# A fused attention and two-MoE kernel: k of the fourth head pair is turned by VectorE, two small opening steps change places or engines, and the last store changes its queue

## The chip, the cores and the metric

The kernel runs on one core of a Trainium2 chip. The time is device microseconds of one execution. Three executions of the kernel before took 952.24, 953.11 and 955.57 us; the median is 953.11 us.

## The reference

There are three stages. First, causal attention with a decay, over 4 batches, 8 heads, 576 positions and a head dimension of 64; then two feed-forward blocks on the 2304 by 512 result.

```
scores = q @ k.T / sqrt(64)
cum    = cumsum(log(clip(f, 1e-4, 1)))            # f: one forget factor per head and position
scores = where(causal, -1e9, scores + cum_i - cum_j)
attn   = softmax(scores);  x = attn @ v           # x becomes 2304 x 512
x      = relu(x @ w_in)**2 @ w_out                # 512 -> 2048 -> 512
out    = (sigmoid(x @ w_gate) * (x @ w_val)) @ w_out2   # 512 -> 1536 -> 512
```

## The kernel before

The 32 heads are worked in 16 pairs (p = 0 to 15), two heads side by side on the 128 partitions. Each fp32 operand is split into a high and a low part, and each product is a sum of matmuls of such parts. q and k must stand with the head dimension on the partitions. For q, TensorE transposes five 128x128 blocks into PSUM (step TQ). For k there are two ways, chosen by the constant TP. Pairs below TP load k as it is, TensorE transposes it (step TK) and ScalarE and VectorE make its high and low part from PSUM (kh and kl "late"). Pairs from TP on load k by four DMAs (L294) that already put 32x32 blocks where they belong; VectorE turns the blocks in place with one instruction (step TKv, L494), and ScalarE and GpSimd make the parts (steps khe and kle). Before the change TP is 4.

The attention is a pipeline written out by hand. The list ORDER (L647) names the steps of one iteration, each with a lag: a step with lag -1 works in iteration `it` on pair it+1. Two tables, `ahead` and `behind` (L675 to 697), hang further work on a step of an iteration. Every engine runs its instructions in that order, and SyncE issues all DMAs in it. PSUM is a ring of four tiles (`ps2`, names pa0 to pa3, two banks each): every transposing step, score step and product takes the next tile of the ring, and waits until the tile's former user is done. TQ takes an extra tile for k where p is below TP (L454).

The steps that matter here, in short: ql and kl make the low parts of q and k on VectorE; S2, S3, S01 and S4 are the score matmuls (L439, L545); R is the row minimum on VectorE (L413), X the exponential on ScalarE (L421), M the scaling on GpSimd (L565); G is the transposing of the weights on TensorE (L576, L582), E its copy out of PSUM; PV is the product with v (L610). In `setup` (L336) f is clamped, its logarithm taken on ScalarE, summed by a scan on VectorE, and split in two parts that are stored in SBUF and sent by DMA (cr_load, L311) to the rows that the score matmuls read.

When the last pairs run out, TensorE fills its gaps with the first four groups of the up product (`fill_mm`, L661, two groups to a ring tile, one in each bank); `up1_post` on ScalarE reads each (Relu, L234; Square, L235). Then the eight PSUM banks are used singly (`hbank`, L730), from bank 0 on, which is the first half of pa0.

At the end, `finish2` (L1502) adds the last products and stores three pieces of the last rows; all by SyncE.

Of the kernel before, what the change touches and what calls it, by code (L numbers as in the profile page):

```python
# [13 lines left out]
AF = mybir.ActivationFunctionType  # L14
ALU = mybir.AluOpType
# [26 lines left out]
def kernel(  # L42
# [13 lines left out]
    nc = tc.nc  # L56
    B, H, S, D = q.shape
# [211 lines left out]
    cum_f = pts[0:BH, 0:S]  # L269
    f_sb = pts[0:BH, S:2 * S]  # L270
    cum_s = pts[0:BH, 2 * S:5 * S].bitcast(F32R)
# [1 line left out]
    cum_b = pts[0:BH, 6 * S:6 * S + 3 * HALF].bitcast(BF16)  # L273

    ring = [0]
    TP = 4

    def k_flat(p):
        return nat["k"][p % 2].rearrange("p c h d -> p (c h d)")[:, 0:S]
# [1 line left out]
    def ps2():  # L281
        ring[0] += 1
        return pair_t[(ring[0] - 1) % 4]

    def load(p, which):
        b, h0 = divmod(2 * p, H)
        for src, nm_ in ((q, "q"), (k, "k"), (v, "v")):
            if nm_ not in which:
                continue
            t = nat[nm_][p % len(nat[nm_])]  # L290
            if nm_ == "k" and p >= TP:
                for r in range(4):
# [43 lines left out]
    def setup():  # L336
        nc.vector.memset(qk[1]["kh"].bitcast(F32)[:, 0:256], 0.0)
        nc.vector.memset(one_l.bitcast(F32), 0.0)
        for r in range(2):
            nc.vector.memset(one_l.bitcast(F32)[64 * r:64 * r + 64, 128 * r:128 * r + 128], 1.0)  # L340
        nc.vector.memset(cum_s.bitcast(F32)[:, 2 * S:3 * S], 0.0)
        for t in sm_t:
            nc.vector.memset(t[:, 9:13], 1.0e-9)
        nc.vector.memset(nm_t[0][:, 9:11], 0.0)
        for r in range(2):
            nc.vector.memset(nm_t[0][64 * r:64 * r + 64, 9 + r:10 + r], 1.0)
        busy(16)
        nc.sync.dma_start(out=f_sb, in_=f.rearrange("b h s -> (b h) s"))
        make_identity(nc, ident)
        for nm_ in "qk":  # L350
            for t in nat[nm_]:
                nc.gpsimd.memset(t[64:128, NF, :, :], 0.0)
        load(0, "qk")
        nc.vector.tensor_reduce(out=nm_t[0][:, 0:1], in_=ident[:, 0:111:22], axis=mybir.AxisListType.X, op=ALU.add)
        nc.vector.tensor_scalar(one_l, one_l.bitcast(F32), nm_t[0][:, 0:1], None, op0=ALU.mult)
        nc.vector.tensor_scalar(f_sb, f_sb, 1.0e-4, 1.0, op0=ALU.max, op1=ALU.min)
        nc.scalar.activation(out=f_sb, in_=f_sb, func=AF.Ln)
        nc.scalar.activation(out=sm_t[0][0:BH, 0:1], in_=f_sb[:, 0:1], func=AF.Exp)
        nc.vector.tensor_tensor_scan(out=cum_f, data0=f_sb, data1=f_sb, initial=0.0, op0=ALU.add, op1=ALU.min)
        nc.scalar.activation(out=cum_s[:, 0:S], in_=cum_f, func=AF.Copy)  # L360
        nc.vector.tensor_tensor(
            out=cum_s[:, S:2 * S], in0=cum_f, in1=cum_s.bitcast(F32)[:, 0:S], op=ALU.subtract
        )
        for d in qk:
            nc.gpsimd.memset(d["cr"].bitcast(F32), 0.0)
        for t in nat["v"]:
            nc.gpsimd.memset(t[64:128, NF, :, :], 0.0)
        for t in pt_t:
            nc.gpsimd.memset(t[:, 2 * POFF[NF] + S:2 * POFF[NF] + PC], 0.0)
        cum_v = cum_s.bitcast(F32).rearrange("p (t s) -> p t s", t=3)  # L370
        load(1, "q")
        cr_load(0, cum_v)
        load(1, "k")
        cr_load(1, cum_v)
        nc.gpsimd.memset(maskc, 0.0)
        nc.gpsimd.affine_select(
            out=maskc[:, MD:MD + 128], in_=maskc[:, MD:MD + 128], pattern=[[-1, 128]],
            compare_op=ALU.is_ge, fill=BIG, base=0, channel_multiplier=1,
        )
        for r in range(2):  # L380
            nc.gpsimd.affine_select(
                out=maskc[64 * r:64 * r + 64, S - REM:S], in_=maskc[64 * r:64 * r + 64, S - REM:S],
                pattern=[[-1, REM]], compare_op=ALU.is_ge, fill=BIG, base=0, channel_multiplier=1,
            )
# [67 lines left out]
    def TQ(p):  # L452
        x = ps2()
        if p < TP:  # L454
            live["kt", p] = ps2()
# [29 lines left out]
    def TK(p):  # L485
        if p >= TP:
            return
# [2 lines left out]
            load(p + 2, "k")  # L490

    def TKv(p, first=False):
        if p >= TP and first == (p < TP + 2):
            nc.vector.transpose(out=k_flat(p), in_=k_flat(p))  # L494
            live["k", p] = k_flat(p)

# [141 lines left out]
    for c in range(9):  # L638
        t = "4" if c == 8 else f"{c // 2}{'ab'[c % 2]}"
# [36 lines left out]
    for m in range(2):  # L676
# [5 lines left out]
        for n in range(4):  # L682
            ahead[b + 6 + n if m == 0 else b + 6, "kle"] = (
                ahead.get((b + 6, "kle"), []) * m + [part_fn(conv_low, m, n)]
            )
    for p in range(TP, TP + 2):
        behind[p - 2, "N0"] = [lambda p=p: TKv(p, True)]
    behind[2, "TK"] = [lambda: w_load("in", 0), lambda: w_load("in", 1)]
    behind[-1, "TQ"] = [lambda: busy(3)]
# [14 lines left out]
    for it in range(min(lags), NP + max(lags)):  # L704
# [6 lines left out]
        for nm_, lag in steps:  # L711
            p = it - lag
# [317 lines left out]
    for i, (k_, jj, w) in enumerate(steps):  # L1030
        if i == NW - 1:
# [12 lines left out]
            for n in range(4):  # L1044
                t = pu_p.tile([128, 4, BT], F32, tag=f"pa{n}", name=f"pa{n}")
# [39 lines left out]
        ws, s = aop[k_, w], gg.pop(i)  # L1085
# [195 lines left out]
    for n, (z, key, m) in enumerate(items):  # L1281
# [12 lines left out]
        elif m % 2:  # L1294
            at(*slot(z + 6), *[part_fn(w_sum, key, m // 2, x) for x in range(4)])
            for x in range(4):
                p = 42 * (m // 2) + x - 1
# [84 lines left out]
    t = wr_p.tile([128, 3584], F32R, tag="r1", name="r1b")  # L1382
# [119 lines left out]
    def finish2(m):  # L1502
# [2 lines left out]
        last = m == wsteps[-1][0]  # L1505
        tl, th = (j * BT + cs.start for j in (j0, j1))

        def store(t, s, lo, hi):
            nc.sync.dma_start(
                out=out[t:t + 128, 256 * lo:256 * hi], in_=r[:, s + lo:s + hi, :].rearrange("p i n -> p (i n)")  # L1510
            )

# [15 lines left out]

        def p4():
            vadd(r[:, 2], two(m, 0)[:, 1], r[:, 2])  # L1530
            store(th, 2, 0, 1)

        def p34():
            vadd(r[:, 1:3], two(m, 3), r[:, 1:3])
# [116 lines left out]
```

## Time and profile before

| what | value |
|---|---|
| median of three executions | 953.11 us |
| the profiled execution | 953.69 us |
| its span, first to last instruction | 951.9 us |
| TensorE matmul busy | 943.2 us (99%), 6255 instructions |
| VectorE, ScalarE, GpSimd busy | 738.1, 560.2, 339.4 us |
| mean granted clock of TensorE | 0.999 |
| DMA | 160.88 MB, 169 GB/s |

The profiled execution is 1.79 us longer than its span. Times below count from the start of the span. A row of a timeline gives the start, the length, the engine, the line of the kernel, what it did, and in brackets how long the engine was idle before it and what ended that. "SPq" is SyncE's queue of DMA issues: the length is that of the issue, not of the transfer. TensorE's weight loads (PEld) run beside its matmuls (PE).

### The profile page before, as it was taken

What the parts mean: (1) busy time and instruction counts of PE and PEld (TensorE: products, weight loads), DVE (VectorE), ACT (ScalarE), POOL (GpSimd) and SP (SyncE); (2) the same over time, 40 slices, a digit from 0 to 9 for tenths busy, and PEclk for the clock granted to TensorE, in tenths of its full rate; (3) what the DMA queues carried; (4) which work ended last, traced back from release to release, by engine and by line L of the source; (5) the groups of instructions that cost most, each with busy time, mean ns of one, the idle gap of its engine ahead of it and who ended that gap; (6) DMA issues with size and microseconds to landing.
All of it is one profiled execution on the core that took longest, in us unless ns stands there. A gap on an engine that the chain in (4) does not pass through costs nothing.

```text
span 951.9 us, 17958 instructions
## 1 busy us (share of the span) xinstructions
PE 943.2 (99%) x6255; PEld 905.7 (95%) x6255; DVE 738.1 (78%) x1467; ACT 560.2 (59%) x1148; POOL 339.4 (36%) x403
## 2 busy tenths in 40 slices
PE   8999999999999999999999999999999999999998
PEld 7888888999999999999999999999999999889998
DVE  7899998277776775787879989767676777698885
ACT  7899998466555756556556566444445455344332
POOL 7798998012021210055023355634243342300000
PEclk9999999999999999999999999999999999999999
DMA  5744430387878988757766513334333345764441
GB/s 121 169 97 97 89 78 15 115 293 249 266 247 279 311 282 296 208 167 208 226 213 204 176 57 103 117 114 138 114 116 128 127 166 201 265 214 143 151 132 69
DMA packets 173635, 160.88 MB, mean 169 GB/s; under 512 B 80328, under 2 KB 150300, under 8 KB 173544
## 3 DMA queue, kind: packets, MB, share of 16 engines
q1 hardware_dynamic: 173544, 159.74, 55.0%
q8 instruction: 49, 0.80, 0.3%
q14 instruction: 42, 0.34, 0.1%
HBM read 102.93 MB, written 56.73 MB: 168 GB/s over the span
## 4 chain that ended last, share of the span: by engine, by line
PE 89%; DVE 4%; DMA 4%; ACT 1%; issue 1%; POOL 1%; SPq 0%; ACTq 0%; DVEq 0%; POOLq 0%
PE ps L1145 28%; PE ps L226 20%; PE ps L1091 10%; PE ps L1491 9%; PE ps L1367 5%; PE pa L610 5%; PE pa L439 4%; PE pa L576 3%; DMA gl<-g 3%; DVE gg L787 2%; PE pa L545 1%; PE pa L395 1%; PE pa L582 1%; PE pa L226 1%; ACT gg L786 1%
## 5 line engine op out<-in xcount | busy, mean ns | idle before, releaser
L226 PE MATMUL ps<-xT,hl 128*128 128x384 f32 x1104 | 191.5, 334 | 0.0
L226 PEld LDWEIGHTS ps<-xT,hl 128*128 128x128 f32 x1104 | 191.4, 188 | 0.0
L1091 PE MATMUL ps<-gg,ao 128*128 128x384 f32 x1008 | 177.6, 335 | 1.5 <-DVE gg L787 1.4
L1091 PEld LDWEIGHTS ps<-gg,ao 128*128 128x128 f32 x1008 | 174.4, 188 | 4.6 <-DVE gg L787 4.4
L565 POOL TENSOR_TENSOR pt<-pt,sm 128x128 f32<-128x128 f32 (+2 forms) x142 | 104.5, 767 | 17.9 <-DVE sm L557 13.8
L787 DVE TENSOR_TENSOR gg<-gl,gg 128x768 fp32r<-128x768 f32 x78 | 85.2, 1099 | 29.3 <-ACT gg L786 28.8
L1145 PE MATMUL ps<-xT,r 128*128 128x384 f32 x576 | 107.6, 334 | 0.0
L786 ACT ACTIVATE gg<-gl 128x768 fp32r<-128x768 f32 x78 | 65.8, 845 | 65.4 <-DMA gl<-g 36.8
L1145 PEld LDWEIGHTS ps<-xT,r 128*128 128x128 f32 x576 | 100.5, 188 | 0.1
L212 DVE TENSOR_TENSOR gt<-gt 128x384 f32<-128x384 f32 x96 | 53.7, 600 | 58.2 <-ACT gt L235 56.0
L421 ACT ACTIVATE pt<-pt,nm 128x384 f32<-128x384 f32 (+2 forms) x144 | 82.8, 579 | 4.4 <-DVE nm L413 4.4
L413 DVE CUSTOM_DVE_ANT_0 pt<-pa,maskc 128x384 f32<-128x384 f32 (+2 forms) x144 | 67.0, 515 | 1.6 <-PE pa L439 1.6
L183 POOL TENSOR_TENSOR hl<-wf,hl 128x512 fp32r<-128x512 f32 x14 | 18.1, 1292 | 125.4 <-ACT hl L179 125.4
L132 ACT ACTIVATE wtmp<-wraw 128x512 f32<-128x512 f32 x66 | 43.9, 665 | 30.5 <-DMA wraw<-in_moe_w_in_dram 12.4
L849 POOL TENSOR_TENSOR xT<-yt,xT 128x384 fp32r<-128x384 f32 x12 | 17.1, 1430 | 122.9 <-ACT xT L845 119.1
L1145 PE MATMUL ps<-xT,f 128*128 128x384 f32 x288 | 55.7, 334 | 0.0
L1145 PE MATMUL ps<-t,r 128*128 128x384 f32 x288 | 54.1, 334 | 0.0
L235 ACT ACTIVATE gt<-gt 128x384 f32<-128x384 f32 x96 | 50.5, 526 | 3.1
L234 ACT ACTIVATE gt<-ps 128x384 f32<-128x384 f32 x92 | 43.9, 477 | 11.7 <-PE ps L226 11.4
L1145 PEld LDWEIGHTS ps<-xT,f 128*128 128x128 f32 x288 | 50.4, 188 | 0.0
L1145 PEld LDWEIGHTS ps<-t,r 128*128 128x128 f32 x288 | 50.3, 188 | 0.1
L155 DVE SCALAR_TENSOR_TENSOR wtmp<-wraw,wtmp 128x512 int32<-128x512 int32 (+1 forms) x68 | 46.5, 684 | 1.6
(259 smaller groups left out, 1935.5 us busy)
## 6 DMA issues: line engine op xcount, KB each, us to landing
gl<-g SPq DMA_DIRECT2D x90, 384.0 KB
g<-gt SPq DMA_DIRECT2D x168, 192.0 KB
wraw<-in_moe_w_out_dram SPq DMA_DIRECT2D x28, 512.0 KB
x<-g SPq DMA_DIRECT2D x72, 128.0 KB
wraw<-in_moe_w_in_dram SPq DMA_DIRECT2D x16, 512.0 KB
wraw<-in_moe_w_val_dram SPq DMA_DIRECT2D x12, 512.0 KB
g<-pb SPq DMA_DIRECT2D x29, 192.0 KB
wraw<-in_moe_w_gate_dram SPq DMA_DIRECT2D x10, 512.0 KB
```

Source lines behind the costliest of these rows:

```text
L212: nc.vector.tensor_tensor(out=t, in0=a, in1=b_, op=ALU.subtract)
L226: nc.tensor.matmul(h, lhsT=a, rhs=xT[c][:, b_, t0:t0 + BT], start=(c == 0 and i == 0), stop=(c == KD - 1 and i == 2))
L235: nc.scalar.activation(out=r, in_=r, func=AF.Square)
L413: nc.vector.tensor_tensor_reduce(out=o, in0=s, in1=mask, scale=1.0, scalar=3.0e38, op0=ALU.add, op1=ALU.min, accum_out=scol(p, nm_t, c),)
L421: nc.scalar.activation(out=x, in_=x, func=AF.Exp, bias=scol(p, nm_t, c), scale=-1.0, accum_out=scol(p, sm_t, c))
L565: nc.gpsimd.tensor_tensor(out=x, in0=x, in1=scol(p, sm_t, c).to_broadcast([128, e - a]), op=ALU.mult)
L610: nc.tensor.matmul(o[64 * h:64 * h + 64, 512 * half + s - lo:512 * half + hi - lo], lhsT=vn[:, c, h, :], rhs=pts[:, h * PW + c * PS + s:h ...
L786: nc.scalar.activation(out=s[:, 0], in_=t, func=AF.Copy)
L787: nc.vector.tensor_tensor(out=s[:, 1], in0=t, in1=s.bitcast(F32)[:, 0], op=ALU.subtract)
L1091: nc.tensor.matmul(o, lhsT=ws[:, a, u, cs], rhs=s[:, b_, u, :], start=(k_ in (0, 2, 5) and w == u == x == 0), stop=(w == NW - 1 and u == 1 ...
L1145: nc.tensor.matmul(o, lhsT=w[p][:, a, ws], rhs=operand(n, jj, b_, c), start=(first and c == x == 0), stop=(c == 1 and x == 2), skip_group_ ...
L1491: nc.tensor.matmul(o, lhsT=YR[i % 4][:, a, FROM[n]], rhs=b_op(n, u, b_), start=(x == u == y == 0), stop=(u == NU2 - 1 and y == 2), skip_gr ...
```

## The change

There are four edits. The clamp of f stands ahead of two small operations on VectorE. The high part of the decay sums is copied by VectorE instead of ScalarE. TP becomes 3, so the fourth pair (p = 3) goes the way of the block loads, and its turn stands in the plain step TKv of iteration 1, while those of pairs 4 and 5 stay where they were (behind N0). The last of the three final stores is issued by ScalarE.

```diff
--- before.py
+++ after.py
@@ -273,7 +273,7 @@
     cum_b = pts[0:BH, 6 * S:6 * S + 3 * HALF].bitcast(BF16)
 
     ring = [0]
-    TP = 4
+    TP = 3
 
     def k_flat(p):
         return nat["k"][p % 2].rearrange("p c h d -> p (c h d)")[:, 0:S]
@@ -351,13 +351,13 @@
             for t in nat[nm_]:
                 nc.gpsimd.memset(t[64:128, NF, :, :], 0.0)
         load(0, "qk")
+        nc.vector.tensor_scalar(f_sb, f_sb, 1.0e-4, 1.0, op0=ALU.max, op1=ALU.min)
         nc.vector.tensor_reduce(out=nm_t[0][:, 0:1], in_=ident[:, 0:111:22], axis=mybir.AxisListType.X, op=ALU.add)
         nc.vector.tensor_scalar(one_l, one_l.bitcast(F32), nm_t[0][:, 0:1], None, op0=ALU.mult)
-        nc.vector.tensor_scalar(f_sb, f_sb, 1.0e-4, 1.0, op0=ALU.max, op1=ALU.min)
         nc.scalar.activation(out=f_sb, in_=f_sb, func=AF.Ln)
         nc.scalar.activation(out=sm_t[0][0:BH, 0:1], in_=f_sb[:, 0:1], func=AF.Exp)
         nc.vector.tensor_tensor_scan(out=cum_f, data0=f_sb, data1=f_sb, initial=0.0, op0=ALU.add, op1=ALU.min)
-        nc.scalar.activation(out=cum_s[:, 0:S], in_=cum_f, func=AF.Copy)
+        nc.vector.tensor_copy(cum_s[:, 0:S], cum_f)
         nc.vector.tensor_tensor(
             out=cum_s[:, S:2 * S], in0=cum_f, in1=cum_s.bitcast(F32)[:, 0:S], op=ALU.subtract
         )
@@ -490,7 +490,7 @@
             load(p + 2, "k")
 
     def TKv(p, first=False):
-        if p >= TP and first == (p < TP + 2):
+        if p >= TP and first == (TP < p < TP + 3):
             nc.vector.transpose(out=k_flat(p), in_=k_flat(p))
             live["k", p] = k_flat(p)
 
@@ -683,7 +683,7 @@
             ahead[b + 6 + n if m == 0 else b + 6, "kle"] = (
                 ahead.get((b + 6, "kle"), []) * m + [part_fn(conv_low, m, n)]
             )
-    for p in range(TP, TP + 2):
+    for p in range(TP + 1, TP + 3):
         behind[p - 2, "N0"] = [lambda p=p: TKv(p, True)]
     behind[2, "TK"] = [lambda: w_load("in", 0), lambda: w_load("in", 1)]
     behind[-1, "TQ"] = [lambda: busy(3)]
@@ -1505,8 +1505,8 @@
         last = m == wsteps[-1][0]
         tl, th = (j * BT + cs.start for j in (j0, j1))
 
-        def store(t, s, lo, hi):
-            nc.sync.dma_start(
+        def store(t, s, lo, hi, eng=nc.sync):
+            eng.dma_start(
                 out=out[t:t + 128, 256 * lo:256 * hi], in_=r[:, s + lo:s + hi, :].rearrange("p i n -> p (i n)")
             )
 
@@ -1528,7 +1528,7 @@
 
         def p4():
             vadd(r[:, 2], two(m, 0)[:, 1], r[:, 2])
-            store(th, 2, 0, 1)
+            store(th, 2, 0, 1, nc.scalar)
 
         def p34():
             vadd(r[:, 1:3], two(m, 3), r[:, 1:3])
```

On VectorE, in iteration 1, between the row minima of pair 1 and the low part of q of pair 2, the change puts this (kn_155 is the tile of k of odd pairs, ql_160 and kl_162 the low parts of pair 2, pt_174 the scores of pair 1):

```order
 L413 ISA pt_174,nm_179<-pa_146,maskc 128x128
 L413 ISA nm_179 128x1
+L494 STREAM_TRANSPOSE kn_155<-kn_155 128x576
 L468 SCALAR_TENSOR_TENSOR ql_160<-pa_147,qh_159 128x576
 L504 TENSOR_TENSOR kl_162<-pa_148,kh_161 128x576
```

One instruction is added; it waits for the four DMAs that load k of pair 3, and ql and kl of pair 2 now stand behind it.

On SyncE, the loads of iterations 0 and 1 (cr_163 is the decay row of pair 2, vn_157 is v of pair 1):

```order
 L304 DMA qn_153<-in_q_dram 64x2x64
 L311 DMA cr_163<-cum_d 6x576
-L300 DMA kn_155<-in_k_dram 128x4x64 x2
-L304 DMA kn_155<-in_k_dram 64x2x64
+L294 DMA kn_155<-in_k_dram 32x18x32 x4
 L300 DMA vn_157<-in_v_dram 128x4x64 x2
 L304 DMA vn_157<-in_v_dram 64x2x64
```

Three issues for k of pair 3 become four; their place in the queue stays the same.

On TensorE, where the fill groups end and the first group in a single bank begins (pa_145 and pa_146 are pa0 and pa1 of the ring, ps_2684 before and ps_2681 now are bank 0). Before:

```order
L226 MATMUL pa_146<-xT_127,hl 128x384 x3
L226 MATMUL pa_146<-xT_128,hl 128x384 x3
L226 MATMUL pa_146<-xT_129,hl 128x384 x3
L226 MATMUL ps_2684<-xT_126,hl 128x384 [waits DVE_49,PE_49]
L226 MATMUL ps_2684<-xT_126,hl 128x384 x2
```

and now:

```order
L226 MATMUL pa_145<-xT_127,hl 128x384 x3
L226 MATMUL pa_145<-xT_128,hl 128x384 x3
L226 MATMUL pa_145<-xT_129,hl 128x384 x3
L226 MATMUL ps_2681<-xT_126,hl 128x384 [waits PE_49,Activation_49]
L226 MATMUL ps_2681<-xT_126,hl 128x384 x2
```

With one ring tile less taken, everything from iteration 2 on sits one tile lower, and the fill groups now lie in pa0, whose first bank is bank 0. The first group there waits for ScalarE now; the count that it waits for is that of the second Relu of the two fill groups.

## Rows read from the trace of the kernel before

**Rows 1.** Chain that ended last, whole run: start us, length us, what worked.

```profile
7.54 2.37 DMA cr<-pts
...
19.09 3.15 POOL pt L565 x3
...
30.70 2.18 PE pa L576 x20
...
177.82 191.36 PE ps L226 x1104
```

**Rows 2.** Busy time by engine in iterations two and three of attention; PEclk is granted clock.

```profile
core 0: us, PE busy (x) PEld busy (x) DVE busy (x) ACT busy (x) POOL busy (x), PEclk, DMA share, GB/s
22.98:33.37 10.39, 10.39 (x106) 8.93 (x106) 8.66 (x29) 8.14 (x25) 7.30 (x11) 1.00 0.69 146
33.37:43.10 9.73, 9.73 (x99) 8.27 (x99) 8.88 (x31) 8.87 (x26) 8.18 (x11) 1.00 0.78 194
```

**Rows 3.** Timeline, VectorE, 16 to 46 us: start, length, line, what; idle before in brackets.

```profile
19.28 0.75 DVE L468 SCALAR_TENSOR_TENSOR ql<-pa,qh 128x576 fp32r<-128x576 f32 x1
...
20.62 0.75 DVE L413 CUSTOM_DVE_ANT_0 pt<-pa,maskc 128x576 f32<-128x576 f32 x1
...
21.29 0.95 DVE L449 COPY pts<-pa 128x768 f32<-128x768 f32 x1
...
33.68 0.78 DVE L494 STREAM_TRANSPOSE kn<-kn 128x576 f32<-128x576 f32 x1
```

**Rows 4.** Timeline, SyncE's DMA issues, 0 to 45 us.

```profile
7.54 0.82 SPq L311 DMA_DIRECT2D cr<-pts  x1
...
13.86 0.61 SPq L304 DMA_DIRECT2D kn<-in_k_dram  x1
...
21.19 0.97 SPq L300 DMA_DIRECT2D kn<-in_k_dram  x2
...
26.67 2.16 SPq L294 DMA_DIRECT2D kn<-in_k_dram  x4
```

**Rows 5.** Timeline, TensorE, 16 to 46 us.

```profile
17.31 0.74 PE L395 MATMUL pa<-ident,kn 128*128 128x128 f32 x5 [0.18 <-DMA kn<-in_k_dram]
...
19.52 2.40 PE L576 MATMUL pa<-ident,pt 128*128 128x128 f32 x20 [0.21 <-DVE nm L413]
...
22.98 0.50 PE L439 MATMUL pa<-cr,one_l 64*128 64x512 f32 x2
```

**Rows 6.** TensorE after its last matmul: stretch, length, busy, granted clock, DMA share, GB/s.

```profile
950.40:950.60 0.20, 0.00 (x0) 0.83 0.63 205
950.60:950.80 0.20, 0.00 (x0) 0.50 0.01 0
```

**Rows 7.** Timeline, TensorE, opening and end of the run.

```profile
1.19 3.78 PE L334 MATMUL pa<-kh 128*128 128x256 f32 x16 [1.19 <-DVE kh L337]
...
944.60 2.28 PE L1491 MATMUL ps<-xT,xT 128*128 128x256 f32 x18
...
947.43 0.87 PE L1491 MATMUL ps<-xT,xT 128*128 128x256 f32 x6
```

**Rows 8.** Timeline, VectorE and ScalarE, opening.

```profile
2.85 0.16 DVE L354 TENSOR_REDUCE nm<-ident 128x1 f32<-128x6 f32 x1
...
3.32 0.54 DVE L356 TENSOR_SCALAR pts<-pts 32x576 f32<-32x576 f32 x1
...
6.00 0.67 ACT L360 ACTIVATE pts<-pts 32x576 fp32r<-32x576 f32 x1
```

**Rows 9.** Timeline, ScalarE, 172 to 181 us.

```profile
177.86 0.49 ACT L234 ACTIVATE gt<-pa 128x384 f32<-128x384 f32 x1 [3.64 <-PE pa L226]
...
178.82 0.47 ACT L234 ACTIVATE gt<-pa 128x384 f32<-128x384 f32 x1
```

**Rows 10.** Tail: last DMA issue on SyncE, and a stretch with its DMA share.

```profile
949.00 0.40 SPq L1509 DMA_DIRECT2D out_dram<-r  x1
...
949.50:950.00 0.50, 0.00 (x0) 0.00 (x0) 0.00 (x0) 0.00 (x0) 0.00 (x0) 1.00 1.04 389
```

## The prediction

> **What bounds the kernel now.** I read the share of busy time first: TensorE is busy for 943.2 of 951.9 us, so a change pays only where TensorE waits or where it has work taken away. Then the chain of waits, in order of time: it runs through TensorE nearly everywhere, from 177.82 us on in one piece of 191.36 us [rows 1]. Only in the opening does it run elsewhere: over the DMA that carries the decay sums (cr, 7.54 us, 2.37 us long) and later over GpSimd's scaling (19.09 us) [rows 1]. All four edits touch the opening, the hand-over to the up product, or the tail. Third, the stretches of iterations 2 and 3: TensorE is busy throughout in both, but iteration 2 takes 10.39 us and iteration 3 takes 9.73 [rows 2]. The difference is the five transposes of k of pair 3. Last, the timelines of VectorE and SyncE around 20 us, because both engines work strictly in order and the change puts a new wait there [rows 3, 4].
>
> The sum is made against the profiled execution, 953.69 us, which lies 0.58 us above the median of 953.11. I take 0.58 off at the end.
>
> **Opening: clamp and copy.** The clamp starts at 3.32 us; two small operations ahead of it start at 2.85 [rows 8]. Ahead of them it gains 0.47 us, if f has landed by then; if f lands only at 3.32, it gains nothing. The copy takes ScalarE 0.67 us [rows 8]. VectorE's price for a copy of this shape isn't in the trace; the clamp on the same 32x576 costs it 0.54 us, which is my value, and a copy as slow as ScalarE's is the other bound. With the hand-over between engines gone this is about 0.13 to 0.2 us. So the issue of cr on SyncE comes 0 to 0.65 us earlier; I take 0.6. SyncE's timeline shows one issue after another, with gaps of 0.1 us at most, from there to the row at 21.19 us [rows 4], so its whole queue moves up by the same 0.6 us. By itself this would be worth 0.6 us. It isn't booked by itself, since the next part decides when TensorE goes on.
>
> **k of pair 3: the new wait.** VectorE reaches the new turn where it began ql of pair 2, at 19.28 us [rows 3], now 18.7. The turn needs the four DMAs of k of pair 3. Their place in SyncE's queue is that of the issue at 21.19 us; four issues of this kind take 2.16 us [rows 4]. So the last issue ends at 21.19 - 0.6 + 2.16 = 22.75. From the end of an issue to the landing the nearest rows give two bounds. cr: 2.37 - 0.82 = 1.55 us [rows 1, 4]. k of pair 2: its last issue ended at 14.47, and TensorE waited for it until 17.31, which makes 2.84 at most [rows 4, 5]. I take 1.7, near cr, since the row of 2.84 may hold other waits too. The landing is then at 24.45, and VectorE stands for some 5.7 us.
>
> Behind the turn on VectorE are ql, kl, the row minimum R4 and the copy E2. In the trace they follow each other by 0.67 us (19.28, then 20.62 and 21.29) [rows 3]. The turn takes 0.78 us [rows 3], so ql ends at 24.45 + 0.78 + 0.75 = 25.98, kl at 26.65, R4 at 27.3. The TensorE steps wait for them through the ring: G2 takes the tile that ql reads, G3 the tile of kl, G4 the tile of R4. So TensorE ends G1 at about 19.6 (start 19.52 - 0.6 [rows 5], six transposes) and stands until 26.0. At 0.109 us for a transpose (2.18 us for 20 [rows 1]) G2 (6), G3 (8, from 26.65) and G4 (5) end at 28.05. Then S3 of pair 1 starts, which started at 22.98 [rows 5]: 5.1 us late.
>
> **The clock after the wait.** TensorE's last matmul ends at 947.43 + 0.87 = 948.30 [rows 7]; the granted clock goes from 1.00 to 0.50, the 1.2 GHz level, around 950.5 [rows 6]. That is 2.2 us of standing; here it stands for 6.4. So I expect G2 to start at half the clock. In the opening, after standing, 16 dummy matmuls of 256 columns took 3.78 us, 0.236 each; at the end 18 of the same width took 2.28 us, 0.127 each [rows 7]. About 3.8 us of half pace is therefore my value for the way back. At 0.218 us for a transpose G2 ends at 27.3, G3 at 29.05, and with the clock back at 29.8 G4 ends at 30.0. S3 is 7.0 us late instead of 5.1; the half clock costs 1.9 us. Its bounds are 0 and, if it stays low through S3 and S2 as well, some 3 us.
>
> The Trainium skill (TensorE: Matmul & The Clock Gate, part 1 on the clock gate) says that the ramp costs under one per cent of a usual kernel and shouldn't be fitted. By that page the term is left out and the whole sum below is 1.9 us smaller; I weigh it as the first rival, at full clock, worked out from the rows above.
>
> **k of pair 3: what goes.** Iteration 2 loses five transposes and becomes like iteration 3: 9.73 - 10.39 = -0.66 us [rows 2]. ScalarE's kh moves to an earlier slot at the same price. GpSimd gets kl of pair 3; it is busy for 7.30 of 10.39 us, and iteration 3 shows the same work done beside a full TensorE at 8.18 of 9.73 [rows 2], so I cost it at nothing. Without that cover it would be under 1 us. The load of k of pair 5 now stands behind two weight loads on SyncE. SyncE can go on issuing while TensorE stands for 6 us, so I cost this at nothing; without the stand it could make VectorE wait, at most for about the 2.16 us of its four issues.
>
> **The ring at the hand-over to the up product.** One ring tile less is taken, so all later tiles shift by one. The last fill groups now lie in pa0, and the first group in single banks (bank 0) waits for ScalarE to read both. Before, this group began at 177.82 without a wait [rows 1]. ScalarE starts the first Relu at 177.86, after waiting for TensorE, and the second at 178.82 for 0.47 us [rows 9]. So TensorE now stands from 177.82 to about 179.3: +1.5 us, in a stage where TensorE has no gap that could take it up. If the first Relu were enough, it would be 0.55; these are the bounds. It is too short to lower the clock by the row above.
>
> **The last store.** SyncE issues it at 949.00 for 0.40 us [rows 10]. ScalarE is idle and could issue 0.2 us earlier; that would give -0.24 with the spacing. But from 949.5 on the 16 DMA engines are at a share of 1.04 [rows 10], busy with the two stores before, so the last byte doesn't come sooner. I take 0, with -0.4 (the whole issue) and +0.4 (an issue as long as cr's 0.82) as bounds.
>
> The Trainium skill (DMA: Bandwidth & Descriptors, "Issuing engines are not separate DMA queues") says that another issuing engine saves only the time of the issue, since all use the same 16 engines. By the issue rows alone this edit gives -0.24, by the page and the share of 1.04 it gives 0; I go by the latter.
>
> **The sum.** +7.0 (S3 late) - 0.66 (transposes) + 1.5 (ring) + 0 (store) = +7.85. 953.69 + 7.85 - 0.58 = 960.95, say 961.0 us.
>
> **Rivals.**
> - The same wait, at full clock: 5.1 - 0.66 + 1.5 = +5.95, which gives 959.05 us. For it: the mean granted clock is 0.999 over the whole run, the opening included, so the opening's slow matmuls are an indirect witness. Against it: the fall at 950.5.
> - A late landing: 2.84 us instead of 1.7, and SyncE's queue doesn't move up by 0.6. That adds 1.75: 962.7 us. For it: 128-byte pieces of k, four times 576 of them. Against it: cr landed in 1.55.
> - No wait (not slower): k of pair 3 lands before VectorE comes to it. Then the opening gives -0.6, the transposes -0.66, the ring +1.5: +0.24, 953.35 us. It decides from a landing at 18.7 us; the issue would have to end at 17.2, and SyncE would have to be 6 us ahead of its trace. Nothing in the rows allows that, unless VectorE were as late itself.
>
> **How the numbers follow.** Forecast 0.55, full clock 0.24, late landing 0.12, no wait 0.07, anything else 0.02. About 0.3% (2.9 us) is what a measurement of this kernel can tell from no change. The first three cases lie above 956.0, so slower has 0.92 with half of the rest; no wait is "same"; for faster, the opening and the transposes would have to be joined by 1.6 us more. The range goes from full clock with the near landing (1.55) and one Relu, 959.05 - 0.15 - 0.95 = 957.95, taken down to 957.0 for an edge of the store and of the opening, up to the late landing with the store's bound, 963.1, taken to 963.5.
>
> **What would show it.** VectorE idle for 5 to 6 us before L494 around 24 us, ended by the DMA of kn; TensorE idle for about 6 us before L576, then a granted clock of 0.5 in the slices from some 22 to 30 us; S3 of pair 1 at 30 us; iterations from 2 on at 9.73 us each; TensorE idle for 1.5 us before the first matmul on ps, ended by ScalarE's L234; DMA share at 1.0 in the last two us as before. I am wrong if VectorE doesn't wait at L494, or if the wait ends at another time than 24 to 26 us; the clock term is wrong if G2 to G4 take 2.1 us instead of 4; the ring term if the first ps matmul follows the fill group at once.

## The result and the profile after

The changed kernel takes 960.32 us (median of 6 executions, 959.68 to 961.12) beside 954.13 us of the kernel before on the same chip. The ratio is 1.0067, with a 95% interval from 1.0051 to 1.0083: slower by 4.9 to 7.9 us. Run once more on another chip it took 959.15 us beside 952.86, ratio 1.0065 (1.0052 to 1.0078). The forecast was 961.0 us. The profiled execution took 961.12 us, with a span of 959.3.

VectorE's timeline after, the rows that answer to [rows 3]:

```profile
18.45 0.08 DVE L413 DVE_READ_ACCUMULATOR2_ANT nm<- 128x1 f32 x1
24.46 0.78 DVE L494 STREAM_TRANSPOSE kn<-kn 128x576 f32<-128x576 f32 x1 [5.92 <-DMA kn<-in_k_dram]
25.16 0.72 DVE L468 SCALAR_TENSOR_TENSOR ql<-pa,qh 128x576 fp32r<-128x576 f32 x1
25.80 0.74 DVE L504 TENSOR_TENSOR kl<-pa,kh 128x576 fp32r<-128x576 f32 x1
27.63 0.96 DVE L449 COPY pts<-pa 128x768 f32<-128x768 f32 x1 [0.41 <-issue]
```

VectorE is free at 18.53 us and stands for 5.92 us before the turn of k of pair 3, until the DMA has brought it. ql, kl and the copy behind it start 5.9 to 6.3 us later than before.

SyncE's queue after, answering to [rows 4]: the decay sums for pair 2, and the four issues of k of pair 3:

```profile
19.20 0.78 SPq L311 DMA_DIRECT2D cr<-cum_d  x1
20.04 2.04 SPq L294 DMA_DIRECT2D kn<-in_k_dram  x4
```

The load stands behind the same transfers as before. The last issue ends at 22.08 us, and VectorE has the data 2.38 us later.

TensorE's timeline after, answering to [rows 5]:

```profile
18.68 0.85 PE L576 MATMUL pa<-ident,pt 128*128 128x128 f32 x6 [0.21 <-DVE nm L413]
26.03 3.22 PE L576 MATMUL pa<-ident,pt 128*128 128x128 f32 x14 [6.50 <-DVE ql L468]
29.04 1.27 PE L582 MATMUL pa<-ident,pt 128*128 128x128 f32 x5
30.24 0.68 PE L439 MATMUL pa<-cr,one_l 64*128 64x512 f32 x2
```

The wait of VectorE is passed on: after six transposes TensorE stands for 6.50 us, until ql has freed the tile of G2. The score step S3 of pair 1 (last row) starts at 30.24 us instead of 22.98.

The same places as stretches (start:end, length, busy time of PE, PEld, DVE, ACT and POOL with instructions, granted clock, DMA share, GB/s), the last two answering to [rows 2]:

```profile
18.68:26.03 7.35, 0.85 (x7) 0.64 (x7) 1.57 (x3) 2.54 (x11) 2.79 (x4) 0.85 0.69 140
26.03:30.24 4.21, 4.21 (x19) 3.88 (x19) 2.40 (x6) 0.96 (x2) 1.91 (x5) 0.50 0.79 150
30.24:40.27 10.03, 10.03 (x99) 8.56 (x99) 8.13 (x29) 8.34 (x26) 7.47 (x10) 0.98 0.23 51
40.27:50.00 9.73, 9.73 (x99) 8.27 (x100) 8.84 (x31) 8.82 (x26) 8.33 (x12) 1.00 0.85 205
```

In the second stretch the granted clock is 0.50, the level of 1.2 GHz: 19 transposes take 4.21 us. Iteration 2 now takes 10.03 us instead of 10.39, with 99 matmuls like iteration 3; a rest of the half clock lies in it (0.98). From iteration 3 on a pass takes 9.73 us, as before.

TensorE's waits after (total, times, longest), the largest four:

```profile
PE pa L576 <- DVE ql L468: 6.5, 1, 6.5
PE ps L226 <- ACT gt L234: 1.5, 1, 1.5
PE pa L334 <- DVE kh L337: 1.2, 1, 1.2
PE ps L1091 <- DVE gg L787: 1.1, 2, 0.7
```

The second one is the hand-over to the up product, which had no wait before [rows 1]. TensorE there, before and then after:

```profile
177.66 14.55 PE L226 MATMUL ps<-xT,hl 128*128 128x384 f32 x83
```

```profile
185.95 4.26 PE L226 MATMUL ps<-xT,hl 128*128 128x384 f32 x23 [1.51 <-ACT gt L234]
```

ScalarE after, answering to [rows 9]:

```profile
184.48 0.49 ACT L234 ACTIVATE gt<-pa 128x384 f32<-128x384 f32 x1 [3.64 <-PE pa L226]
185.43 0.47 ACT L234 ACTIVATE gt<-pa 128x384 f32<-128x384 f32 x1
```

The first matmul on a single bank starts when the second Relu has read (185.43 + 0.47 = 185.90).

The opening on VectorE after, answering to [rows 8]:

```profile
2.85 0.61 DVE L354 TENSOR_SCALAR pts<-pts 32x576 f32<-32x576 f32 x1
5.59 0.45 DVE L360 CAST pts<-pts 32x576 fp32r<-32x576 f32 x1
```

The clamp starts 0.47 us earlier, and the copy takes 0.45 us instead of ScalarE's 0.67 [rows 8]. The issue of cr, at 7.54 us before [rows 4], is at 6.90.

The end of the program, answering to [rows 10]: ScalarE's queue, and the DMA engines (their share of time is the last column but one):

```profile
956.12 0.38 ACTq L1509 DMA_DIRECT2D out_dram<-r  x1
```

```profile
956.50:957.00 0.50, 0.00 (x0) 0.00 (x0) 0.00 (x0) 0.00 (x0) 0.00 (x0) 1.00 0.82 279
957.00:957.50 0.50, 0.00 (x0) 0.00 (x0) 0.00 (x0) 0.00 (x0) 0.00 (x0) 1.00 1.01 379
```

Going through the starts of the stages, after minus before: S3 of pair 1 +7.26 us, the first matmul on ps 185.95 - 177.66 = +8.3, the first of L1091 377.42 - 369.02 = +8.4, the first of L1145 554.64 - 547.95 = +6.7, the span +7.4. So the stage of L1091 took 1.7 us less than before in these two profiles, and 0.7 us of that was lost again behind L1145. That was in no term of the forecast; the experiments come back to it.

### The profile page after: what moved, and what is told of

Read it like the earlier page. It is cut to its first block, busy times and chain, and to the rows that moved or that the text cites. A ratio compares the mean times of both kernels' runs of the same rounds, so it can differ in the third digit from the quotient of the medians.

```text
span 959.3 us, 17949 instructions
## 1 busy us (share of the span) xinstructions
PE 943.8 (98%) x6250; PEld 907.6 (95%) x6250; DVE 739.4 (77%) x1468; ACT 560.1 (58%) x1147; POOL 341.9 (36%) x404
## 4 chain that ended last, share of the span: by engine, by line
PE 91%; DMA 3%; DVE 2%; ACT 1%; issue 0%; POOL 0%; SPq 0%; ACTq 0%; DVEq 0%; POOLq 0%
PE ps L1145 27%; PE ps L226 20%; PE ps L1091 14%; PE ps L1491 9%; PE pa L610 5%; PE pa L576 4%; PE pa L439 4%; PE ps L1367 4%; DMA gl<-g 3%; PE pa L545 1%; DVE gg L787 1%; PE pa L582 1%; PE pa L226 1%; PE pa L395 1%; ACT gg L786 1%; PE pa L534 1%
## 5 line engine op out<-in xcount | busy, mean ns | idle before, releaser
L1091 PE MATMUL ps<-gg,ao 128*128 128x384 f32 x1008 | 176.1, 335 | 1.3 <-DVE gg L787 1.1
L1091 PEld LDWEIGHTS ps<-gg,ao 128*128 128x128 f32 x1008 | 174.5, 188 | 2.7 <-DVE gg L787 2.6
L1145 PE MATMUL ps<-xT,r 128*128 128x384 f32 x576 | 107.5, 334 | 0.0
L787 DVE TENSOR_TENSOR gg<-gl,gg 128x768 fp32r<-128x768 f32 x78 | 84.4, 1090 | 28.7 <-ACT gg L786 28.3
L786 ACT ACTIVATE gg<-gl 128x768 fp32r<-128x768 f32 x78 | 66.0, 846 | 63.5 <-DMA gl<-g 38.7
L1145 PEld LDWEIGHTS ps<-xT,r 128*128 128x128 f32 x576 | 100.5, 188 | 0.1
L1145 PE MATMUL ps<-xT,f 128*128 128x384 f32 x288 | 55.7, 334 | 0.0
L1145 PE MATMUL ps<-t,r 128*128 128x384 f32 x288 | 54.1, 334 | 0.0
L1145 PEld LDWEIGHTS ps<-xT,f 128*128 128x128 f32 x288 | 50.4, 188 | 0.0
L1145 PEld LDWEIGHTS ps<-t,r 128*128 128x128 f32 x288 | 50.3, 188 | 0.1
```

Source lines behind the costliest of these rows:

```text
L786: nc.scalar.activation(out=s[:, 0], in_=t, func=AF.Copy)
L787: nc.vector.tensor_tensor(out=s[:, 1], in0=t, in1=s.bitcast(F32)[:, 0], op=ALU.subtract)
L1091: nc.tensor.matmul(o, lhsT=ws[:, a, u, cs], rhs=s[:, b_, u, :], start=(k_ in (0, 2, 5) and w == u == x == 0), stop=(w == NW - 1 and u == 1 ...
L1145: nc.tensor.matmul(o, lhsT=w[p][:, a, ws], rhs=operand(n, jj, b_, c), start=(first and c == x == 0), stop=(c == 1 and x == 2), skip_group_ ...
```

## The experiments

Each kernel is timed beside the kernel before on one chip. A difference in us below is between the medians of two kernels that were timed beside each other; the interval is that of the ratio.

**1. The three other edits, without the turn of k of pair 3.**

```diff
-    TP = 3
+    TP = 4
-        if p >= TP and first == (TP < p < TP + 3):
+        if p >= TP and first == (p < TP + 2):
-    for p in range(TP + 1, TP + 3):
+    for p in range(TP, TP + 2):
```

> The changed kernel with VectorE turning no k of pair 3 (TensorE transposes it as before): only the clamp's place, the copy of the running sums' high part and the last store are changed. Theory: no wait at the turn, no half clock, no ring wait; the opening's 0.6 us earlier start is what is left: 953.5 us beside 954.1 of the kernel before. Rival (the 6 us lie in the other three edits): 957 or more.

Measured: 954.48 us beside 954.93, ratio 0.9993 (0.9984 to 1.0003). No wait at a turn, no half clock, no wait before ps; S3 of pair 1 at 22.31 us, 0.67 earlier than before. The clamp, the copy and the store together gain about 0.5 us, which these executions can't tell from nothing. The 6 us lie in the fourth pair.

**2. The last store alone by ScalarE, all else as before.**

```diff
-        def store(t, s, lo, hi):
-            nc.sync.dma_start(
+        def store(t, s, lo, hi, eng=nc.sync):
+            eng.dma_start(
...
-            store(th, 2, 0, 1)
+            store(th, 2, 0, 1, nc.scalar)
```

> The kernel before with only the last store issued by ScalarE instead of SyncE. Theory: the issue comes 0.2 us earlier, but the transfer's tail ends where it did: no change, within 0.1 us of 954.1. Rival (the store's issue is on the path to the end): -0.2, and a wait of ScalarE's queue on its first use of it could make it +1.

Measured: 952.97 us beside 953.05, ratio 0.9999 (0.9990 to 1.0008). The end of the program isn't set by when this store is issued.

**3. k of pair 3 loaded earlier.** SyncE issues it right behind the store of the running sum; the load of v of pair 0 goes behind.

```diff
-    behind[0, "S3"] = [lambda: load(3, "q"), lambda: cr_load(2, cum_d), lambda: load(3, "k")]
+    behind[0, "S3"] = [lambda: load(3, "q"), lambda: cr_load(2, cum_d), lambda: load(0, "v")]
+    behind[0, "TK"] = [lambda: load(3, "k")]
-        if 0 <= it < 3:
+        if 1 <= it < 3:
```

> The changed kernel with the load of k of pair 3 issued by SyncE earlier, right behind the store of the running sum, and the load of v of pair 0 later. Theory: VectorE's turn of k finds its data, no 5.9 us wait there, TensorE doesn't stand 6.5 us and its granted clock stays 1.00; what is left is the earlier opening (-0.6), the transposes gone (-0.66) and the ring wait (+1.5): before +0.24, so about 954.4 us beside 954.1 of the kernel before; S3 of pair 1 at about 22.4. Rival (the turn costs by VectorE's own time, or the TensorE clock falls for another reason): a part of the 7.3 us stays, 957 or more.

Measured: 956.18 us beside 954.93, ratio 1.0007 (0.9995 to 1.0018). VectorE's turn in this kernel, and TensorE behind it:

```profile
19.81 0.78 DVE L494 STREAM_TRANSPOSE kn<-kn 128x576 f32<-128x576 f32 x1 [1.13 <-DMA kn<-in_k_dram]
```

```profile
21.38 1.73 PE L576 MATMUL pa<-ident,pt 128*128 128x128 f32 x14 [1.71 <-DVE ql L468]
```

The wait falls from 5.92 to 1.13 us, TensorE stands for 1.71 instead of 6.50, the granted clock of the profiled execution is 1.000, and 5 of the 6 us are gone. Only the places of two loads were changed for that. The theory holds but for a rest: the data came 1.1 us after VectorE, S3 of pair 1 starts at 23.59 us and not at 22.4. Nor did the clock stay up in every execution: in seven of the eleven its mean is 0.997 or 0.998 (median 956.5 us), in the other four 1.000 (955.3); of the 29 executions of the kernel before beside them one has less than 0.999. Only one of the four was profiled, so how long TensorE stood in the seven is not shown.

**4. The tile that shifts the PSUM ring.** The changed kernel leaves one extra tile out of the ring; here the ring is moved on by one at that place, so that all later steps get the banks that they had before.

```diff
         if p < TP:
             live["kt", p] = ps2()
+        elif p == TP:
+            ring[0] += 1
```

> The changed kernel with one tile of the transposes' pool left out of the turn where the first k turned by VectorE stands, so that from there on the PSUM banks fall to the same operations as in the kernel before. Theory (three terms: the wait at VectorE's turn of k of pair 3 with the half clock, 7.3 us; five TensorE transposes gone, -0.66; the wait of the first ps matmul for ScalarE, 1.5): that wait of 1.51 us goes and nothing takes its place, total 1.5 below the changed kernel, about 958.8 us beside 960.3, stage start S3 of pair 1 still at 30.2. Rival (the wait is slack that a later stage fed by DMA gives back anyway): 960.3 as the changed kernel, with the stage of line 1091 longer by 1.5.

Measured: 960.35 us beside 954.93, ratio 1.0057 (1.0044 to 1.0071). The wait before the first matmul on ps is gone, but the stage of L1091 took 179.1 us in this profile, after 177.2 in that of the changed kernel, and the two kernels had stood on different chips. So both were run once more, on one chip:

> The changed kernel once more, to stand beside the others on one chip: 6 to 6.5 us above the kernel before, a wait of 1.5 us before the first matmul on ps, VectorE's turn of k of pair 3 at 24.0 to 24.5 us. The stalls in the stage of line 1091 (1.1 us in its first profile, 0.5 to 2.9 in the others) come out otherwise in each execution.

> The kernel with one tile of the pool left out once more, beside the changed kernel on one chip. Theory (the wait of 1.5 us before the first matmul on ps is a loss): 1.5 below the changed kernel. Rival (the stage of line 1091 gives it back, since its stalls shrink when it begins later): 0 to 0.7 below it, with a longer stage of line 1091.

Measured: 959.15 us without and 958.46 us with the tile moved on, ratios to the kernel before of 1.0065 (1.0052 to 1.0078) and 1.0053 (1.0041 to 1.0066). The first matmul on ps starts at 185.55 us (after a wait of 1.51) and at 184.16 (no wait, the row below), the stage of L1091 takes 177.5 and 177.4 us, and the spans are 958.6 and 957.0 us. In the profiles the wait costs its full 1.5 us; the medians, 0.7 apart with overlapping intervals, are too coarse to show it by themselves.

```profile
184.16 8.13 PE L226 MATMUL ps<-xT,hl 128*128 128x384 f32 x46
```

**5. Both: the earlier load and the tile moved on.**

> Both edits: k of pair 3 loaded earlier, and the one tile left out. Theory: only the gains stay, -0.6 of the opening and -0.66 of the transposes, 1.26 us below the kernel before, about 952.9 us beside 954.1. Rival (the end is set by stages fed by DMA, which give back what the front gains): 954.1, as before, with the stage of line 1091 or 1145 longer by what the front gained.

Measured: 953.77 us beside 954.93, ratio 0.9990 (0.9977 to 1.0004), 2.4 us below experiment 3 on the same chip. At the first matmul on ps the two profiles are 1.73 us apart (180.16 and 178.43): 1.51 are the wait before ps, and a wait of TensorE at 51 us is 0.56 in experiment 3 and 0.23 here. Another 1.1 us lie in the stage of L1091 (179.2 and 178.1). VectorE still waits for k of pair 3, for 0.68 us. Three of the twelve executions have a mean clock of 0.996 to 0.998 and take 955.8 to 958.1 us; the median of the other nine is 953.6.

**6. The turn at another place of VectorE's order.** It stands behind N0, as for pairs 4 and 5; the load is where the change put it.

```diff
-        if p >= TP and first == (TP < p < TP + 3):
+        if p >= TP and first == (p < TP + 3):
-    for p in range(TP + 1, TP + 3):
+    for p in range(TP, TP + 3):
         behind[p - 2, "N0"] = [lambda p=p: TKv(p, True)]
```

> The changed kernel with VectorE's turn of k of pair 3 put behind the same operation as its siblings, after the q and k of the running pair have been scaled. Theory: VectorE comes to the turn at about 21.9 us and waits about 2.6 for the same landing at 24.5, but TensorE's G2, G3, G4 have what they wait for, so that TensorE stands for 1 to 2 us only and doesn't lose the clock: with the ring wait (1.5), the opening (-0.6) and the transposes (-0.66) before +2 to +3, about 956 to 957 us. Rival (the landing itself holds the pass, wherever the turn stands): about 960.

Measured: 954.10 us beside 953.05, ratio 1.0008 (0.9999 to 1.0017).

```profile
24.12 0.78 DVE L494 STREAM_TRANSPOSE kn<-kn 128x576 f32<-128x576 f32 x1 [2.34 <-DMA kn<-in_k_dram]
```

```profile
18.77 2.40 PE L576 MATMUL pa<-ident,pt 128*128 128x128 f32 x20 [0.20 <-DVE nm L413]
25.66 2.93 PE L610 MATMUL pa<-pts,vn 128*64 128x256 f32 x28 [0.74 <-DVE pts L449]
```

The data lands when it did, but ql, kl and R4 stand ahead of the wait now. TensorE runs its 20 transposes in one piece and loses 0.74 us behind the turn instead of 6.50. So it was not the late load by itself that cost 6 us; it was the late load with everything that TensorE needed queued behind it. The first matmul on ps is 2.4 us later than in the kernel before, as the forecast of +2 to +3 has it; in the median only 1.0 us of that arrives.

**7. The clock.** To keep TensorE busy while it waits, 50 matmuls of 256 columns were added behind G1, into unused columns of the tile that G2 takes.

```diff
+    def warm_pe(n):
+        w = qk[0]["kh"]
+        for _ in range(n):
+            nc.tensor.matmul(pair_t[2][:, 640:896], lhsT=w[:, 0:128], rhs=w[:, 0:256], start=True, stop=True)
+    behind[1, "G1"] = [lambda: warm_pe(50)]
```

> The changed kernel with 50 further matmuls of 256 columns on TensorE behind G1 of the first pass of the first loop, into columns that nothing reads, so that TensorE is busy while it waits for VectorE's turn of k of pair 3. Theory (of the 7.3 us about 2.0 are the half clock that follows the standing): the wait at the turn stays, the granted clock stays 1.00, the work from 26.0 us to S3 of pair 1 takes about 2.1 us instead of 4.2, total 2 below the changed kernel, about 958.3 us beside 960.3. Rival (the wait alone costs 7.3 and the clock is made up by other waits): 960.3; if the added matmuls run on past the landing they cost their own time on top.

Measured: 964.55 us beside 953.05, ratio 1.0120 (1.0105 to 1.0135). This missed its aim: the added matmuls wait for ql as well, since they write to a tile whose former user is ql.

```profile
25.26 7.96 PE L678 MATMUL pa<-kh 128*128 128x256 f32 x50 [5.74 <-DVE ql L468]
```

In the second attempt 90 matmuls of 128 columns write into the tile of G1 itself.

```diff
+            nc.tensor.matmul(live["g", 1, 0][:, 896:1024], lhsT=w[:, 0:128], rhs=w[:, 0:128], start=True, stop=True)
+    behind[1, "G1"] = [lambda: warm_pe(90)]
```

> The changed kernel with 90 further matmuls of 128 columns on TensorE behind G1 of the first pass of the first loop, into columns of G1's own tile that nothing reads, so that they wait for nothing that VectorE does behind its turn. Theory (2.0 of the 7.3 us are the half clock that follows the standing): TensorE is busy from 18.7 to about 24.6 us, the granted clock stays 1.00, the 19 transposes from 26.0 us on take 2.2 us instead of 4.2, S3 of pair 1 at 28.2 instead of 30.2: total 2 below the changed kernel run beside it. Rival (the clock falls for another reason, or the wait's end is all that counts): the same total, or longer by what the added matmuls run past the wait.

Measured: 961.60 us beside 952.86, ratio 1.0087 (1.0073 to 1.0100), 2.45 us above the changed kernel on the same chip. TensorE in this kernel, and the stretch of G2 to G4:

```profile
19.31 10.25 PE L678 MATMUL pa<-kh 128*128 128x128 f32 x90
29.39 1.72 PE L576 MATMUL pa<-ident,pt 128*128 128x128 f32 x14
```

```profile
29.39:31.58 2.19, 2.19 (x21) 2.02 (x21) 1.21 (x3) 1.79 (x5) 0.00 (x0) 1.00 0.70 144
```

The same stretch in the changed kernel that was run beside it:

```profile
25.06:29.28 4.22, 4.22 (x20) 3.89 (x21) 2.40 (x6) 0.96 (x2) 1.92 (x5) 0.50 0.74 140
```

The added matmuls took 0.112 us each (90 from 19.31 to 29.39 us), where I had counted on 90 in some 5.9 us, and ran 4.1 us past the end of the wait (ql starts at 24.44 us; in the changed kernel G2 starts 0.87 after it, here at 29.39 instead of 25.31). But TensorE didn't stand, the clock stayed at 1.00 (2.4 GHz), and the same 19 transposes took 2.19 us instead of 4.22. That makes the half clock worth 2.03 us. The parts add up: +4.08 of overrun, -2.03 of clock, +0.24 of a later landing (23.74 after 23.50) give +2.29 at S3 of pair 1, and 31.58 - 29.28 = 2.30 is read there. The next pass takes 9.85 us with the full clock and 10.31 in the changed kernel, so that the half clock has a tail of up to 0.46 us more. The first matmul on ps is 1.84 us later, the median 2.45.

**8. A version without the losses.** Experiments 3, 4 and 6 together: earlier load, the turn behind N0, the tile moved on.

> The changed kernel with k of pair 3 loaded earlier, VectorE's turn of it behind the same operation as its siblings, and the one tile of the pool left out. Theory: k has landed at about 19.8 us (as with the earlier load alone), VectorE comes to the turn at about 21.8 us, so nothing waits; first matmul on ps at about 176.4 us, 1.3 before the kernel before, total 1.3 lower. Rival (the stage of line 1091, whose stalls differ from one execution to the next, gives back what the front gains): no change, its own stalls longer by 1 us.

Measured: 952.72 us beside 952.86, ratio 0.9995 (0.9986 to 1.0004). S3 of pair 2 is 1.0 us earlier than before, at 32.38, but the gain is lost in the fourth pass, at the turn of k of pair 5:

```profile
44.11 0.78 DVE L496 STREAM_TRANSPOSE kn<-kn 128x576 f32<-128x576 f32 x1 [1.85 <-DMA kn<-in_k_dram]
```

```profile
35.48 1.14 SPq L118 DMA_DIRECT2D wraw<-in_moe_w_in_dram  x2
36.73 3.75 SPq L294 DMA_DIRECT2D kn<-in_k_dram  x4
```

With TP = 3 that load stands behind two weight loads, since it now follows GpSimd's kl of pair 3. The last edit puts the weights behind it:

```diff
-    behind[2, "TK"] = [lambda: w_load("in", 0), lambda: w_load("in", 1)]
+    behind[2, "kle"] = [lambda: w_load("in", 0), lambda: w_load("in", 1)]
```

> The kernel with the earlier load of k of pair 3, its turn behind the usual operation and one tile left out, and now the two weight loads issued behind the load of k of pair 5 instead of ahead of it. Theory (what is left of the loss there is VectorE's 1.85 us wait for k of pair 5, which passes 0.98 and 0.70 us on to TensorE and makes the fourth pass 11.7 us long): the wait goes, the pass takes about 9.75 us, first matmul on ps at about 176.7 us instead of 178.6, total 1 to 1.3 below the kernel before. Rival (the load of k of pair 5 is late for the DMA engines' sake and not for its place behind the weights): the wait stays and the total is as without this edit, 0.1 below the kernel before.

Measured: 951.45 us (11 executions, 950.19 to 952.04) beside 953.08, ratio 0.9985 (0.9976 to 0.9994). It is faster than the kernel before by 0.6 to 2.3 us, and by the two ratios (0.9985 and 1.0065 of some 953 us) 7.6 us faster than the changed kernel.

```profile
42.27 0.78 DVE L496 STREAM_TRANSPOSE kn<-kn 128x576 f32<-128x576 f32 x1
48.71 0.78 DVE L496 STREAM_TRANSPOSE kn<-kn 128x576 f32<-128x576 f32 x1 [1.07 <-DMA kn<-in_k_dram]
```

```profile
44.55 0.34 PE L439 MATMUL pa<-cr,one_l 64*128 64x384 bf16 x2 [0.76 <-DMA cr<-cum_d]
```

The wait for k of pair 5 is gone, so the queue place was its cause. But the pass took 10.67 us and not 9.75: the next transfers are late instead (cr by 0.76 us, k of pair 6 by 1.07). The first matmul on ps starts at 177.56 us, only 0.10 earlier than in the kernel before. The expected size was wrong there. In the profiles the span is 2.3 us shorter than before (949.6 beside 951.9), and 2.1 of these lie in the stage of L1091; so what makes this version faster than the kernel before is not shown.

**What stays open.** The stage of L1091, the product of the first block's hidden values with w_out, is the only later one whose length differs by more than 1 us between the profiles. TensorE waits in it for VectorE's part of splitting the hidden values (gg, L787), a few times for 0.2 to 0.8 us. VectorE waits for ScalarE's part (L786), and ScalarE most of all for the values themselves, which were stored to DRAM and are loaded back (gl). The profile of the kernel before gives the busy time, the mean ns of one, the idle time ahead of them and what ended most of it:

```profile
L787 DVE TENSOR_TENSOR gg<-gl,gg 128x768 fp32r<-128x768 f32 x78 | 85.2, 1099 | 29.3 <-ACT gg L786 28.8
L786 ACT ACTIVATE gg<-gl 128x768 fp32r<-128x768 f32 x78 | 65.8, 845 | 65.4 <-DMA gl<-g 36.8
```

So the stage is fed by loads, and when they land bears on its length. Its length, beside what each kernel gained or lost ahead of it:

| kernel | first ps, minus 177.66 | median, minus before beside it | stage of L1091 |
|---|---|---|---|
| before | 0 | 0 | 178.9 |
| store alone | 0.0 | -0.1 | 177.8 |
| TP = 4 | -0.4 | -0.4 | 181.3 |
| changed, twice | +8.3, +7.9 | +6.2, +6.3 | 177.2, 177.5 |
| tile moved on, twice | +6.5, +6.5 | +5.4, +5.6 | 179.1, 177.4 |
| earlier load | +2.5 | +1.2 | 179.2 |
| earlier load, tile | +0.8 | -1.2 | 178.1 |
| turn behind N0 | +2.4 | +1.0 | 177.3 |
| added matmuls, twice | +13.1, +9.7 | +11.5, +8.7 | 176.0, 176.1 |
| all three | +0.9 | -0.1 | 177.1 |
| all three, weights later | -0.1 | -1.6 | 176.9 |

In the kernels with TP = 3 the time comes out 0.9 to 2.1 us better than the start of the up product would have it; in those with TP = 4 it doesn't. A later start isn't the reason, as the last row shows: it begins that stage when the kernel before does. What in the load of a fourth pair by blocks reaches a stage 200 us later, no run here shows. The profiles are one execution each, and the length spreads by more than the effect (177.8 to 181.3 with TP = 4), so the table is a hint from the medians, not a finding. No run here changes these loads.

## Why the prediction came out right

- **What bounds the kernel, and where the change acts.** Right. Experiment 1 puts all of the loss in the fourth pair, experiment 3 takes 5 of the 6 us away by an earlier load alone.
- **Opening.** Forecast 0.6 us with the copy at 0.54. The copy took 0.45, cr was issued 0.64 earlier. That SyncE's whole queue moves up by the same amount failed: k of pair 3 began at 20.04 us instead of 21.19 [rows 4], 1.15 earlier. The store of the running sum, ahead of the loads of q and cr, had already moved up by 0.82 (17.61 to 16.79), and the issues of q behind that took 0.99 us where they had taken 1.32, so some issues ahead of it took less time than in the kernel before; the forecast had kept their lengths.
- **The wait at the turn.** Forecast: landing at 24.45 us, TensorE standing until 26.0, S3 at 30.0. Read: 24.46, 26.03, 30.24. That the landing was hit to 0.01 us is luck, two errors that cancel: the issue ended 0.67 earlier than forecast (22.08, not 22.75) and the landing took 2.38 us instead of 1.7. In the second profile of the same kernel it took 1.74 (issue from 19.72 to 21.76, landing 23.50), and TensorE stood for 5.52 us. So the forecast had the end of the issue 0.7 to 1.0 us too late, and S3 is 6.3 to 7.3 us late. In the nine profiles in which VectorE waits for k of pair 3, it has the data 1.68 to 2.38 us after the last issue; 1.7 is at the low end. The rival of a late landing had its 2.84 us from a load of another shape. That the row held other waits as well, as the forecast supposed, isn't shown: TensorE stood there for 0.18 us, ended by that very load [rows 5].
- **The clock.** Forecast 1.9 us; experiment 7 measures 2.03. The clock fell to 0.50 while TensorE stood and came back some 4.6 us after it began again. The forecast's 3.8 came from slow matmuls in the opening, for which the profile gives a granted clock of 1.00 (1.19 to 4.97 us of the kernel before); the rows don't show that these ran at half the clock. The rival at full clock, 959.05 us, is refuted as a mechanism, though its time lies nearer to the second median than the forecast does. The Trainium skill (TensorE: Matmul & The Clock Gate, part 1 on the clock gate) says that the ramp costs under one per cent of a typical kernel's span, and that a model shouldn't be fitted to a specific count of slow matmuls. The trace agrees with the size, 2.03 of 960 us being 0.2%. That the term is to be left out of a sum is the forecast's reading of it; for one edit this would be wrong here, since the term is more than a quarter of the delay of S3.
- **The transposes.** Forecast -0.66 by making iteration 2 like iteration 3. It has 99 matmuls now and took 10.03 us, with 0.3 of half clock in it; the passes behind it take 9.73.
- **The cover for k of pair 5.** It was costed at nothing, with the note that without the stand it could make VectorE wait for up to 2.16 us. Right in both parts: the changed kernel shows no such wait, experiment 8, where TensorE no longer stands, shows one of 1.85. In experiments 3 and 6 the wait comes one pair later (k of pair 6, 1.13 and 1.16 us) and passes 0.56 and 0.86 us on to TensorE at 51 us.
- **The ring.** Forecast 1.5 us, ended by the second Relu; read 1.51 in both profiles, and gone in both profiles of experiment 4; the medians on one chip differ by 0.7 us only.
- **The last store.** Forecast 0, measured -0.1 (experiment 2). The store is issued 0.2 us sooner after the last addition, but the DMA engines have a share of 1.01 from 957.0 to 957.5 us, and the span ends 3.7 us behind TensorE's last matmul as it did before (3.6).
- **The sum.** Forecast +7.85; the two profiles show +8.3 and +7.9 at the start of the up product, so the terms are right to 0.5 us. In the time +6.2 and +6.3 arrived. Of the missing 1.6 to 2.1 us the profiles show 1.7 and 1.4 in the stage of L1091, which the sum took as unchanged; the cause is open, and the spread of single executions is as large (the first profile is the longest of its six, 961.12 us). That the forecast of 961.0 us came within 0.7 of the measured 960.32 is in part luck: it started from 953.11 us, and the kernel before took 954.13 when it was timed beside the changed one.
- **No wait.** The rival of +0.24 us had a condition, k landing before 18.7 us. The early load came within 1.1 us of that in experiment 3 and 0.7 in experiment 5. That experiment 5 came out at -1.2, beside -1.26 by the same terms without the ring's 1.5, is a coincidence: VectorE still waited, the first matmul on ps was 0.8 us late, and the interval of the ratio includes no change. In experiment 8 VectorE doesn't wait for k of pair 3, and S3 of pair 2 is 1.0 us earlier than before, near the 1.26.

## What to carry to other kernels

An instruction that waits for a DMA holds up all that stands behind it on its engine, as ql, kl and R4 stood behind the turn here: before moving one, list what another engine needs from the rows below, and compare the end of the load's issue plus its landing with the time at which the engine arrives. Here either an earlier load or a place further down (behind ql, kl, R4 and the copy behind them) took away 5 of 6 us, and only the second kept the mean clock at 0.999 or more in all its executions. Leaving a tile out of a ring of buffers shifts all later users of the ring; here the price, 1.51 us, stood 160 us later, where the next pool begins. If a shift isn't wanted, skip the slot.

## What the runs showed of the hardware that was not expected

- The clock follows late. Stretches of the changed kernel, with the same columns as above:

```profile
22.00:23.00 1.00, 0.00 (x0) 0.00 (x0) 0.00 (x0) 0.00 (x0) 0.00 (x0) 1.00 0.77 125
23.00:24.00 1.00, 0.00 (x0) 0.00 (x0) 0.00 (x0) 0.00 (x0) 0.00 (x0) 0.91 0.84 174
24.00:30.00 6.00, 3.97 (x19) 3.92 (x19) 3.97 (x8) 0.72 (x1) 1.74 (x5) 0.50 0.76 152
30.00:31.00 1.00, 1.00 (x8) 0.67 (x8) 0.65 (x1) 1.00 (x4) 0.92 (x2) 0.68 0.67 151
```

  TensorE had stood since 19.53 us, and the clock was at 1.00 until some time after 23. It then stayed at 0.50 until about 30.6 (a mean of 0.68 from 30 to 31), for 4.6 us of full work. So it fell some 4.3 us after TensorE's last matmul (a mean of 0.91 from 23 to 24); at the end of the kernel before it fell 2.2 us after it [rows 6, 7]. A wait of 1.71 us (the profile of experiment 3) left the clock at 1.00.
- A matmul of 128 columns on this operand took 0.112 us (experiment 7), about as long as one of 256 columns in [rows 7] (0.127) and as a transpose of 128 columns in [rows 1] (0.109).
- With two loads of weights ahead of them, the four issues of k of pair 5 lasted 3.75 us (experiment 8), and VectorE had the data 3.6 us after the last of them. With the weights behind them, in the last version, they lasted 2.16 us:

```profile
35.73 2.16 SPq L294 DMA_DIRECT2D kn<-in_k_dram  x4
```
